# A two-layer tanh product turned inside out: weight blocks outside, 512-token blocks inside

## The chip, the cores and the metric

One Trainium2 chip, one of its eight cores. The metric is the device time of one execution in microseconds (us); lower is better. The core has a matmul engine (PE, with its weight loads shown as PEld), a vector engine (DVE), a scalar engine (ACT), a general engine (POOL) and a sync engine (SP) that issues the DMAs here. PE adds into PSUM, which has eight banks of 512 fp32 columns for each of 128 partitions; everything else lies in SBUF or in device memory.

## The reference

Attention over 4 batches, 8 heads, 576 tokens and 64 columns a head, then two MoE-like products over the 2304 tokens of all batches:

```python
x = attention(q, k, v, s)                        # 2304 x 512
gate = 1 / (1 + exp(-(x @ w_gate)))              # 512 -> 1536
y = (gate * (x @ w_val)) @ w_out                 # 1536 -> 512
h = y @ w_in                                     # 512 -> 2048   (the tanh product)
out = (h - tanh(h)) @ w_out2                     # 2048 -> 512
```

## The kernel before, in words

All is fp32. For the large products each operand is split into a high part, rounded to the matmul's type, and a low part, the rest; a product is then three matmuls: high by high, low weight by high tokens, high weight by low tokens. Weights arrive as 64-bit numbers and are converted on chip (`Conversion`: ACT scales the upper words into `tmp`, DVE joins the lower words in, lines 82 and 83, ACT writes the high part, line 124, POOL the low part, line 114; each `tick` does one step of three blocks that follow each other). Matmuls of 128 rows by 128 weight columns stream the tokens as columns; every one has a weight load of its own.

The order of work on each engine is the order in which the program writes it (`manual_schedule`); an engine runs its instructions in that order, and SP its DMAs. Waits between engines follow from the tiles that instructions write and read.

The stages, in order:

1. Attention, with the first half of the first MoE (gate and value, `gscr` in device memory) worked in between, to 536.9 us.
2. The first MoE's output product, `y`. The loop runs over six blocks of 384 tokens, inside over 12 weight blocks `won`: 72 steps of 12 matmuls. `gload` fetches a tile of gated values four steps ahead, `gsplit` splits it two steps ahead (ACT line 730, DVE line 731). Four PSUM banks collect a block and the next block uses the other four. At a block's end ACT copies them to `y`, which holds all tokens in fp32 (line 796). In this stage the 16 blocks of `w_in` are also converted, into `big`, where all of them stay.
3. The tanh product. The loop runs over eight blocks of 288 tokens, inside over 16 weight blocks: 128 steps of `hmm`, each 12 matmuls into one of the eight banks in turn, then tanh by ACT (line 829), the difference by DVE (line 830) and a store to `g2scr`. `ysplit` splits the next block of `y`, out of SBUF, half a block ahead (lines 773 and 774). `w_out2` is converted here in eight pairs (`PairConversion`, 120 steps spread over 104 steps of the loop); three pairs stay on chip in `WO`, five go to device memory through `wst` and come back as `wload`.
4. The last product, by a seven-multiplication scheme over halves: 40 steps (`dsteps`) of five token blocks by eight pairs of weight blocks. `sload` fetches the tanh product's rows back from `g2scr` (line 854), `sprep` makes seven combinations `sh` and `sl` in slots of one tile each (POOL lines 867 and 869, DVE 868, 871, 872 and 874, ACT 870 and 873), and 42 matmuls of 256 columns follow (lines 957 to 959; 21 of them in the last block). Seven banks collect; `drain` adds them up and stores. `sprep` runs two steps ahead of its use and `sload` two further.

In stage 3 the loads `wload` of pairs 3 and 4 are issued at steps 118 and 122, into the memory of `big`; pairs 5, 6 and 7 follow after the first three steps of stage 4. The buffers of stage 4 lie where `y` was (`d_open`).

Of the kernel before, what the change touches and what calls it, by code (L numbers as in the profile page):

```python
# [16 lines left out]
NT, DM = B * S, H * D  # L17
KD = DM // 128
M1, M2 = 1536 // 128, 2048 // 128
BLK = 384  # L20
NBLK = NT // BLK
Q0 = (0, 128, 256, 384, 448)
GRP = ((0, 256, (0, 1)), (256, 320, (2, 3, 4)))
MASK = -(2.0 ** 33)
# [13 lines left out]
TR2 = 16  # L38
MP = M2 // 2
ND = 3  # L40
HBLK = 288
NHB = NT // HBLK
TB = 256
DG = 2
NSB = -(-(NT // 2) // TB)
# [18 lines left out]
def attention_moe_moe2(ctx: ExitStack, tc: tile.TileContext, kqT, v, s, wg, wv, wo, win, wo2, out):  # L64
# [8 lines left out]
    def bank(i, shape):  # L73
        return psum.tile(shape, F, tag=f"bank{i}", name=f"bank{i}")
# [644 lines left out]
    def gload(i):  # L719
        if i < len(order):  # L720
            blk, m = order[i]
            G_[i] = gs.tile([128, BLK], F, tag="g", name="g", bufs=5)
            SP.dma_start(out=G_[i], in_=gscr[m][:, blk * BLK:(blk + 1) * BLK])

    def gsplit(i):
        if i < len(order):
            raw = G_[i]
            gh = gs.tile([128, BLK], R, tag="gh", name="gh")
            gl = gs.tile([128, BLK], R, tag="gl", name="gl")
# [18 lines left out]
    a_left.close()  # L748

    w2 = ctx.enter_context(tc.tile_pool(name="w2", bufs=1, side="left"))  # L750
    big = [w2.tile([128, 2, 7, 256], R, tag=f"w{q}", name=f"big{q}") for q in range(MP - ND)]

    def win_part(k):
        return big[k // 7].rearrange("p a b c -> p (a b c)")[:, (k % 7) * 512:(k % 7) * 512 + 512]

    winn = [[win_part(2 * m + p) for p in range(2)] for m in range(M2)]
    ys = ctx.enter_context(tc.tile_pool(name="ys", bufs=2, side="left"))
    y_left = ExitStack()
    yp = y_left.enter_context(tc.tile_pool(name="yp", bufs=1, side="left"))
    y = yp.tile([128, KD, NT], F, name="y")  # L760
    jobs = [(win[m].bitcast(U).rearrange("p k c -> p (k c)"), *winn[m]) for m in range(M2)]
    cv3 = b_right.enter_context(tc.tile_pool(name="cv3", bufs=2, side="right"))
    cvt = Conversion(cv3, jobs, 2, 3)
    Y_ = {}

    def ysplit(blk):
        if blk < NHB:
            Y_[blk] = []
            for d in range(KD):
                yh = ys.tile([128, HBLK], R, tag=f"yh{d}", name="yh")  # L770
                yl = ys.tile([128, HBLK], R, tag=f"yl{d}", name="yl")
                src = y[:, d, blk * HBLK:(blk + 1) * HBLK]
                ACT.activation(out=yh, in_=src, func=AF.Copy)
                DVE.tensor_tensor(out=yl, in0=src, in1=yh.bitcast(F), op=ALU.subtract)
                Y_[blk].append((yh, yl))

    for i, (blk, m) in enumerate(order):
        if m == 0:
            acc = [bank(4 * (blk % 2) + d, [128, BLK]) for d in range(KD)]
        gload(i + 4)  # L780
        gsplit(i + 2)
        gh, gl = G_.pop(i)
        for d in range(KD):
            c = slice(d * 128, d * 128 + 128)
            PE.matmul(acc[d], won[m][0][:, c], gh, start=(m == 0), stop=False)  # L785
            PE.matmul(acc[d], won[m][1][:, c], gh, start=False, stop=False)  # L786
        for d in range(KD):
            c = slice(d * 128, d * 128 + 128)
            PE.matmul(acc[d], won[m][0][:, c], gl, start=False, stop=(m == M1 - 1))  # L789
        if i % 3 == 2:  # L790
            cvt.tick()
        if i == len(order) - 3:
            ysplit(0)
        if m == M1 - 1:
            for d in range(KD):
                ACT.activation(out=y[:, d, blk * BLK:(blk + 1) * BLK], in_=acc[d], func=AF.Copy, scale=0.5)
    cvt.finish(len(cvt.jobs) - 1)
    b_right.close()


    wd = ctx.enter_context(tc.tile_pool(name="wd", bufs=1, side="right"))
    fp = ctx.enter_context(tc.tile_pool(name="fp", bufs=2, side="right"))
    c_right = ExitStack()
    cv4 = c_right.enter_context(tc.tile_pool(name="cv4", bufs=2, side="right"))
    WO = {p: wd.tile([128, 2, 7, 256], R, tag=f"w{p}", name=f"wo2{p}") for p in range(ND)}
    DP = {}
    S_ = {"i": 0}
# [4 lines left out]
        w = cv4.tile([128, 2, 7, 256], R, tag="wst", name="wst", bufs=1)  # L812
        return w[:, 0], w[:, 1], lambda: SP.dma_start(out=w2scr[p], in_=w.bitcast(F))

    order = [(blk, m) for blk in range(NHB) for m in range(M2)]

    def hmm(i):
        blk, m = order[i]
        ps = bank(i % 8, [128, HBLK])
        wh, wl = winn[m]  # L820
        for k in range(KD):
            c = slice(k * 128, k * 128 + 128)
            PE.matmul(ps, wh[:, c], Y_[blk][k][0], start=(k == 0), stop=False)  # L823
            PE.matmul(ps, wl[:, c], Y_[blk][k][0], start=False, stop=False)  # L824
        for k in range(KD):
            c = slice(k * 128, k * 128 + 128)
            PE.matmul(ps, wh[:, c], Y_[blk][k][1], start=False, stop=(k == KD - 1))  # L827
        th = fp.tile([128, HBLK], F, tag="th2", name="th2", bufs=6)
        ACT.activation(out=th, in_=ps, func=AF.Tanh)  # L829
        DVE.tensor_tensor(out=th, in0=ps, in1=th, op=ALU.subtract)  # L830
        SP.dma_start(out=g2scr[m][:, blk * HBLK:(blk + 1) * HBLK], in_=th)

    def dwidth(s):
        return min(TB, NT // 2 - s * TB)

    def d_open():
        y_left.close()
        DP["g"] = ctx.enter_context(tc.tile_pool(name="dg", bufs=2, side="left"))
        DP["s"] = ctx.enter_context(tc.tile_pool(name="ds", bufs=2, side="right"))
        for i in range(DG):  # L840
            sload(i)
# [34 lines left out]
        S_["s", i] = sh, sl  # L876

    def wload(p):
        WO[p] = w2.tile([128, 2, 7, 256], R, tag=f"w{p - ND}", name=f"wo2{p}")
        SP.dma_start(out=WO[p].bitcast(F), in_=w2scr[p])  # L880

    cvt = PairConversion(cv4, [("right", [wo2[m * 128:(m + 1) * 128].bitcast(U) for m in (p, p + MP)], p)
                               for p in range(MP)], dst, POOL)
    n0, n1 = 4, len(order) - M2 - 4
    for i, (blk, m) in enumerate(order):
        hmm(i)
        if m == M2 // 2:
            ysplit(blk + 1)
        if n0 <= i < n1:
            for _ in range((i + 1 - n0) * len(cvt.steps) // (n1 - n0) - (i - n0) * len(cvt.steps) // (n1 - n0)):  # L890
                cvt.tick()
        if i == n1:
            cvt.finish(MP - 1)
            cvt.keep()
            c_right.close()
        if i == len(order) - M2 - 2:
            d_open()
        if i == len(order) - 8 or i == len(order) - 4:
            sprep()
        if blk == NHB - 1:  # L900
            if m in (6, 10):
                wload(ND + (m == 10))


    dsteps = [(s, p) for s in range(NSB) for p in range(MP)]
# [102 lines left out]
```

## Time and profile before

| | us |
|---|---|
| median of 3 runs (lowest, highest) | 1080.03 (1079.19, 1080.19) |
| profiled execution, its time | 1079.23 |
| its span, first to last instruction | 1077.3 |
| mean granted PE clock in the profile, share of full | 0.995 |
| start of stage 2, 3, 4 (first matmul) | 536.92, 686.92, 890.45 |

The time of an execution and its span differ by 1.9 us, which lie around the instructions that the profile records. PE is busy in 97% of the span; "busy" there includes the pipelined end of each matmul, so that the durations of single matmuls overlap, and the time from one start to the next is what one costs.

### The profile page before, as it was taken

How to read it: one execution, taken by the hardware profiler on the slowest of the kernel's cores; microseconds unless marked ns; L12 is line 12 of the kernel's file. 1: busy time of each engine (PE TensorE's matmuls, PEld its weight loads, DVE VectorE, ACT ScalarE, POOL GpSimd, SP SyncE). 2: the span in 40 equal slices, each digit the busy share in tenths (PEclk: the TensorE clock that was granted, in tenths of full speed). 3: DMA queues.
4: the chain of work that ended last, by engine and by line, in shares of the span. 5: the costliest groups of instructions: out<-in, count | busy, mean ns of one | idle time of the engine just before them, and what ended most of it. 6: DMA issues, size and time to landing. Idle time of an engine off the chain costs nothing.

```text
span 1077.3 us, 22002 instructions
## 1 busy us (share of the span) xinstructions
PE 1042.4 (97%) x7612; PEld 1016.4 (94%) x7612; DVE 670.7 (62%) x1635; ACT 546.8 (51%) x1289; POOL 462.2 (43%) x606
## 2 busy tenths in 40 slices
PE   7888999999999999999999999999999999999997
PEld 5787999898999999989999999999999999999997
DVE  6786566777776777654545652254454446777875
ACT  6776466666665666643445443344444433433332
POOL 3676465666566566632402210033333314263442
PEclk9999999999999999999999999999999999999999
DMA  6774446657564656615465543245357589534433
GB/s 205 225 237 111 116 135 186 178 152 169 143 178 132 169 153 163 136 41 189 157 208 183 177 153 96 77 133 171 132 196 281 195 294 344 177 108 148 140 96 99
DMA packets 119790, 177.24 MB, mean 165 GB/s; under 512 B 16960, under 2 KB 98368, under 8 KB 118400
## 3 DMA queue, kind: packets, MB, share of 16 engines
q1 hardware_dynamic: 119680, 175.85, 53.9%
q8 instruction: 60, 0.98, 0.4%
q14 instruction: 50, 0.41, 0.1%
HBM read 128.79 MB, written 47.00 MB: 163 GB/s over the span
## 4 chain that ended last, share of the span: by engine, by line
PE 84%; DVE 5%; issue 3%; DMA 3%; ACT 3%; POOL 1%; SPq 0%; POOLq 0%; DVEq 0%; ACTq 0%
PE bank L526 8%; PE bank L527 8%; PE bank L530 8%; PE bank L824 6%; PE bank L827 6%; PE bank L823 6%; PE bank L959 5%; PE bank L958 5%; PE bank L467 5%; PE bank L957 5%; PE bank L785 5%; PE bank L789 5%; PE bank L786 5%; PE bank L428 4%; PE bank L372 2%
## 5 line engine op out<-in xcount | busy, mean ns | idle before, releaser
L959 PE MATMUL bank<-wo,sl 128*128 128x256 f32 x504 | 142.6, 283 | 0.8 <-DVE sl L872 0.8
L957 PE MATMUL bank<-wo,sh 128*128 128x256 f32 x504 | 141.9, 281 | 0.2 <-ACT sh L870 0.2
L958 PE MATMUL bank<-wo,sh 128*128 128x256 f32 x504 | 141.8, 281 | 0.0
L823 PE MATMUL bank<-yh,big 128*128 128x288 f32 x512 | 139.6, 294 | 0.0
L824 PE MATMUL bank<-yh,big 128*128 128x288 f32 x512 | 139.6, 295 | 0.0
L446 ACT ACTIVATE pth<-bank 128x512 fp32r<-128x512 f32 (+2 forms) x128 | 59.5, 465 | 145.1 <-PE bank L467 86.5
L830 DVE TENSOR_TENSOR th<-bank,th 128x288 f32<-128x288 f32 x128 | 57.6, 456 | 113.6 <-ACT th L829 112.6
L447 DVE TENSOR_TENSOR ptl<-bank,pth 128x512 fp32r<-128x512 f32 (+2 forms) x128 | 66.6, 521 | 67.6 <-PE bank L467 35.5
L829 ACT ACTIVATE th<-bank 128x288 f32<-128x288 f32 x128 | 51.9, 410 | 101.3 <-PE bank L827 97.6
L398 ACT ACTIVATE sp<-sp,nm 128x576 f32<-128x576 f32 (+2 forms) x160 | 95.6, 598 | 7.6 <-DVE nm L391 7.5
L959 PEld LDWEIGHTS bank<-wo,sl 128*128 128x128 f32 x504 | 95.3, 189 | 1.8 <-DVE sl L872 1.0
L824 PEld LDWEIGHTS bank<-yh,big 128*128 128x128 f32 x512 | 96.1, 188 | 0.0
L823 PEld LDWEIGHTS bank<-yh,big 128*128 128x128 f32 x512 | 96.0, 187 | 0.0
L957 PEld LDWEIGHTS bank<-wo,sh 128*128 128x128 f32 x504 | 95.3, 189 | 0.4 <-ACT sh L870 0.4
L958 PEld LDWEIGHTS bank<-wo,sh 128*128 128x128 f32 x504 | 95.3, 189 | 0.0
L428 PE MATMUL bank<-ident,sp 128*128 128x128 f32 (+1 forms) x480 | 74.1, 263 | 20.3 <-POOL sp L414 7.8
L867 POOL TENSOR_TENSOR s<-g 128x256 f32<-128x256 f32 (+1 forms) x40 | 37.4, 934 | 125.9 <-DMA g<-h 103.4
L827 PE MATMUL bank<-yl,big 128*128 128x288 f32 x512 | 88.6, 294 | 0.0
L731 DVE TENSOR_TENSOR gl<-g,gh 128x384 fp32r<-128x384 f32 x72 | 40.0, 557 | 75.9 <-PE bank L789 48.1
L428 PEld LDWEIGHTS bank<-ident,sp 128*128 128x128 f32 (+1 forms) x480 | 51.8, 140 | 32.7 <-POOL sp L414 14.5
L730 ACT ACTIVATE gh<-g 128x384 fp32r<-128x384 f32 x72 | 37.3, 529 | 80.6 <-PE bank L786 73.9
L414 POOL TENSOR_SCALAR sp<-sp,r 128x512 f32<-128x512 f32 (+1 forms) x90 | 57.1, 635 | 48.6 <-DVE r L407 34.6
(377 smaller groups left out, 3207.4 us busy)
## 6 DMA issues: line engine op xcount, KB each, us to landing
h<-th SPq DMA_DIRECT2D x128, 144.0 KB, 2.2
kq<-in_kq SPq DMA_DIRECT2D x32, 448.0 KB, 4.0
raw<-in_wo SPq DMA_DIRECT2D x28, 512.0 KB, 4.8
g<-g SPq DMA_DIRECT2D x72, 192.0 KB, 2.6
g<-h SPq DMA_DIRECT2D x72, 128.0 KB, 2.4
w<-wst SPq DMA_DIRECT2D x5, 1792.0 KB, 6.4
wo<-w SPq DMA_DIRECT2D x5, 1792.0 KB, 8.2
cbc<-cum SPq DMA_DIRECT2D x32, 256.0 KB, 5.5
```

The costliest lines, as they stand in the source:

```text
L398: ACT.activation(out=e["sp"], in_=e["sp"], func=AF.Exp, scale=-1.0, bias=e["m"], accum_out=e["sum"])
L428: PE.transpose(ps[:, j, :], e["sp"][p0:128, c:c + 128], ident[p0:128, p0:128])
L447: DVE.tensor_tensor(out=pl[:, js, o:o + n], in0=e["tr"], in1=ph[:, js, o:o + n].bitcast(F), op=ALU.subtract)
L526: PE.matmul(ps, wh[:, c], xh[:, k], start=(k == 0), stop=False)
L527: PE.matmul(ps, wl[:, c], xh[:, k], start=False, stop=False)
L530: PE.matmul(ps, wh[:, c], xl[:, k], start=False, stop=(k == KD - 1))
L823: PE.matmul(ps, wh[:, c], Y_[blk][k][0], start=(k == 0), stop=False)
L824: PE.matmul(ps, wl[:, c], Y_[blk][k][0], start=False, stop=False)
L827: PE.matmul(ps, wh[:, c], Y_[blk][k][1], start=False, stop=(k == KD - 1))
L957: PE.matmul(o, sh[:, g, c], w[:, 0, f], start=(p == 0 and t == 0), stop=False)
L958: PE.matmul(o, sh[:, g, c], w[:, 1, f], start=False, stop=False)
L959: PE.matmul(o, sl[:, g, c], w[:, 0, f], start=False, stop=(p == MP - 1 and t == nt - 1))
```

## The change

Stage 2 takes its tokens in blocks of 512 (four of them and one of 256), 60 steps instead of 72. Its banks are drained straight into the split form: ACT writes the high part out of PSUM with the scale 0.5, DVE the rest out of PSUM; `y` in fp32, `ysplit` and its tiles are gone, and the split `y` of all tokens stays on chip (`Y_`). Of `w_in` four blocks are converted in stage 2 (six ticks), into a ring of four.

Stage 3 has the weight blocks outside and the five token blocks inside (for the last two weight blocks the token blocks are outside and the two weights inside): 80 steps instead of 128. The 12 later ticks of the conversion stand behind the second token block of each weight block from the second on; each overwrites the ring's slot of the weight block that ended before. The weight blocks come in the order 0, 8, 1, 9, ..., so that the pairs which stage 4 needs first are done first. The 120 steps of `PairConversion` are spread over 62 steps instead of 104. `d_open` stands at step 68, `sprep` as before 8 and 4 steps from the end, and the loads of pairs 3 to 6 at steps 72, 74, 76 and 78, each into the memory of a token block of `Y_` that is read no more, pair 7 behind the last step, into the ring's memory. Tiles of stage 4's sums move to other memory. Stages 1 and 4 are otherwise as they were.

The diff, cut:

```diff
-BLK = 384
-NBLK = NT // BLK
+BLK = 512
+BLKS = [(a, min(BLK, NT - a)) for a in range(0, NT, BLK)]
+NBLK = len(BLKS)
+NW = 4
...
-    big = [w2.tile([128, 2, 7, 256], R, tag=f"w{q}", name=f"big{q}") for q in range(MP - ND)]
...
-    winn = [[win_part(2 * m + p) for p in range(2)] for m in range(M2)]
-    ys = ctx.enter_context(tc.tile_pool(name="ys", bufs=2, side="left"))
-    y_left = ExitStack()
-    yp = y_left.enter_context(tc.tile_pool(name="yp", bufs=1, side="left"))
-    y = yp.tile([128, KD, NT], F, name="y")
-    jobs = [(win[m].bitcast(U).rearrange("p k c -> p (k c)"), *winn[m]) for m in range(M2)]
-    cv3 = b_right.enter_context(tc.tile_pool(name="cv3", bufs=2, side="right"))
+    Y_ = []
+    for blk in range(NBLK - 1):
+        yt = w2.tile([128, 2, KD, BLK], R, tag=f"w{blk}", name=f"y{blk}")
+        Y_.append([[yt[:, p, d] for d in range(KD)] for p in range(2)])
+    yt = [[w2.tile([128, 2, 256], R, tag=f"o{p}{d}", name=f"y4{p}{d}") for d in range(2)] for p in range(2)]
+    Y_.append([[yt[p][d // 2][:, d % 2] for d in range(KD)] for p in range(2)])
+    ring = w2.tile([128, NW, 2, 512], R, tag="ring", name="ring")
+    MO = [m for p in range(MP) for m in (p, p + MP)]
+    cv_left = ExitStack()
+    cv3 = cv_left.enter_context(tc.tile_pool(name="cv3", bufs=2, side="left"))
+    jobs = [(win[m].bitcast(U).rearrange("p k c -> p (k c)"), ring[:, j % NW, 0], ring[:, j % NW, 1])
+            for j, m in enumerate(MO)]
     cvt = Conversion(cv3, jobs, 2, 3)
-    Y_ = {}
-
-    def ysplit(blk):
-        if blk < NHB:
-            Y_[blk] = []
-            for d in range(KD):
-                yh = ys.tile([128, HBLK], R, tag=f"yh{d}", name="yh")
-                yl = ys.tile([128, HBLK], R, tag=f"yl{d}", name="yl")
-                src = y[:, d, blk * HBLK:(blk + 1) * HBLK]
-                ACT.activation(out=yh, in_=src, func=AF.Copy)
-                DVE.tensor_tensor(out=yl, in0=src, in1=yh.bitcast(F), op=ALU.subtract)
-                Y_[blk].append((yh, yl))
...
+        w = BLKS[blk][1]
         if m == 0:
-            acc = [bank(4 * (blk % 2) + d, [128, BLK]) for d in range(KD)]
+            acc = [bank((1 + 4 * (blk % 2 == 0) + d) % 8, [128, w]) for d in range(KD)]
...
-        if i % 3 == 2:
+        if i % 8 == 5 and cvt.ticks < NW + 2:
             cvt.tick()
-        if i == len(order) - 3:
-            ysplit(0)
         if m == M1 - 1:
             for d in range(KD):
-                ACT.activation(out=y[:, d, blk * BLK:(blk + 1) * BLK], in_=acc[d], func=AF.Copy, scale=0.5)
-    cvt.finish(len(cvt.jobs) - 1)
+                yh, yl = (Y_[blk][p][d] for p in range(2))
+                ACT.activation(out=yh, in_=acc[d], func=AF.Copy, scale=0.5)
+                DVE.scalar_tensor_tensor(out=yl, in0=acc[d], scalar=0.5, in1=yh.bitcast(F),
+                                         op0=ALU.mult, op1=ALU.subtract)
...
-    order = [(blk, m) for blk in range(NHB) for m in range(M2)]
+    order = [(j, blk) for j in range(M2 - 2) for blk in range(NBLK)]
+    order += [(j, blk) for blk in range(NBLK) for j in (M2 - 2, M2 - 1)]
 
     def hmm(i):
-        blk, m = order[i]
-        ps = bank(i % 8, [128, HBLK])
-        wh, wl = winn[m]
+        j, blk = order[i]
+        a, w = BLKS[blk]
+        ps = bank((i + 1) % 8, [128, w])
+        wh, wl = (ring[:, j % NW, p] for p in range(2))
+        yh, yl = Y_[blk]
         for k in range(KD):
...
-        th = fp.tile([128, HBLK], F, tag="th2", name="th2", bufs=6)
+            PE.matmul(ps, wh[:, c], yl[k], start=False, stop=(k == KD - 1))
+        th = fp.tile([128, BLK], F, tag=f"th{i % 6}", name="th2")[:, :w]
         ACT.activation(out=th, in_=ps, func=AF.Tanh)
         DVE.tensor_tensor(out=th, in0=ps, in1=th, op=ALU.subtract)
-        SP.dma_start(out=g2scr[m][:, blk * HBLK:(blk + 1) * HBLK], in_=th)
+        SP.dma_start(out=g2scr[MO[j]][:, a:a + w], in_=th)
...
     def d_open():
-        y_left.close()
+        cv_left.close()
...
     def wload(p):
-        WO[p] = w2.tile([128, 2, 7, 256], R, tag=f"w{p - ND}", name=f"wo2{p}")
+        WO[p] = w2.tile([128, 2, 7, 256], R, tag=f"w{p - ND}" if p < MP - 1 else "ring", name=f"wo2{p}")
         SP.dma_start(out=WO[p].bitcast(F), in_=w2scr[p])
...
-    for i, (blk, m) in enumerate(order):
+    n0, n1 = 4, 66
+    n2 = len(order) - 2 * NBLK
+    for i, (j, blk) in enumerate(order):
         hmm(i)
-        if m == M2 // 2:
-            ysplit(blk + 1)
+        if i < n2 and blk == 1 and j >= 1 and wcv.ticks < M2 + 2:
+            wcv.tick()
...
-        if i == len(order) - M2 - 2:
+        if i == n1 + 2:
...
-        if blk == NHB - 1:
-            if m in (6, 10):
-                wload(ND + (m == 10))
+        if i > n2 and (i - n2) % 2 == 0:
+            wload(ND + (i - n2) // 2 - 1)
...
-            R_["c1"] = otile("yh6", w)
+            R_["c1"] = otile("o00", w)
             ACT.activation(out=R_["c1"], in_=a, func=AF.Copy)
         elif n == 2:
-            ostore(s, True, 0, dadd(("yh0", "yh1")[par], a, R_["c1"], w), w)
+            ostore(s, True, 0, dadd(("th0", "th1")[par], a, R_["c1"], w), w)
...
+    wload(MP - 1)
     for i, (s, p) in enumerate(dsteps):
...
         sprep()
-        if i + ND + 2 < MP:
-            wload(i + ND + 2)
```

## Rows read from the trace of the kernel before

**Rows 1.** The page's part 1: busy time, share of the span, instructions.

```profile
PE 1042.4 (97%) x7612; PEld 1016.4 (94%) x7612; DVE 670.7 (62%) x1635; ACT 546.8 (51%) x1289; POOL 462.2 (43%) x606
```

**Rows 2.** Windows of three stages and four saturated microseconds; columns in the first line.

```profile
core 0: us, PE busy (x) PEld busy (x) DVE busy (x) ACT busy (x) POOL busy (x), PEclk, DMA share, GB/s
560.00:685.00 125.00, 125.00 (x723) 125.00 (x722) 63.35 (x91) 54.40 (x111) 20.04 (x15) 1.00 0.46 138
711.00:887.00 176.00, 176.00 (x1330) 176.00 (x1329) 78.17 (x169) 75.67 (x167) 55.45 (x47) 1.00 0.58 203
904.00:908.00 4.00, 4.00 (x36) 4.00 (x35) 2.81 (x5) 1.80 (x2) 0.78 (x2) 1.00 1.01 393
910.00:1040.00 130.00, 130.00 (x1098) 130.00 (x1097) 102.62 (x126) 49.25 (x55) 57.22 (x53) 1.00 0.49 150
```

**Rows 3.** Waits of the matmul engine from 495 us: total, times, longest.

```profile
PE bank L959 <- DVE sl L872: 0.8, 1, 0.8
```

**Rows 4.** Timeline of PE where stages meet: start, us, engine, line, shapes.

```profile
536.92 0.33 PE L785 MATMUL bank<-gh,wo0h 128*128 128x384 f32 x1
...
537.72 0.44 PE L785 MATMUL bank<-gh,wo0h 128*128 128x384 f32 x1
...
686.92 0.30 PE L823 MATMUL bank<-yh,big 128*128 128x288 f32 x1
...
890.45 0.28 PE L957 MATMUL bank<-wo,sh 128*128 128x256 f32 x1
```

**Rows 5.** Timeline of PE in attention: a 512-wide matmul and its follower, twice.

```profile
211.15 0.39 PE L373 MATMUL bank<-kl,qs 128*128 128x512 f32 x1
211.38 0.28 PE L526 MATMUL bank<-xh,w03h 128*128 128x256 f32 x1
...
301.86 0.39 PE L373 MATMUL bank<-kl,qs 128*128 128x512 f32 x1
302.08 0.31 PE L526 MATMUL bank<-xh,w06h 128*128 128x320 f32 x1
```

**Rows 6.** Groups by form, first MoE's output product (536.9 to 686.9 us).

```profile
L731 DVE TENSOR_TENSOR gl<-g,gh 128x384 fp32r<-128x384 f32 x70 | 38.9, 557 | 72.3 <-PE bank L789 48.1 <-ACT gh L730 24.1
L730 ACT ACTIVATE gh<-g 128x384 fp32r<-128x384 f32 x69 | 35.9, 530 | 79.3 <-PE bank L786 73.9 <-DMA g<-g 4.6 <-PE bank L789 0.8
...
L114 POOL TENSOR_TENSOR big<-tmp,big 128x512 fp32r<-128x512 f32 x16 | 21.3, 1333 | 97.3 <-ACT big L124 97.3
...
L78 ACT ACTIVATE tmp<-raw 128x512 f32<-128x512 f32 x16 | 10.5, 659 | 0.6 <-DMA raw<-in_win 0.5
L124 ACT ACTIVATE big<-tmp 128x512 fp32r<-128x512 f32 x16 | 9.9, 616 | 0.0
```

**Rows 7.** Groups by form, tanh product (686.9 to 890.4 us).

```profile
L829 ACT ACTIVATE th<-bank 128x288 f32<-128x288 f32 x127 | 51.5, 410 | 100.1 <-PE bank L827 96.4 <-DMA h<-th 3.5
...
L774 DVE TENSOR_TENSOR yl<-y,yh 128x288 fp32r<-128x288 f32 x28 | 13.4, 540 | 0.0
```

**Rows 8.** Groups by form, 512 wide out of PSUM (0 to 536 us).

```profile
L447 DVE TENSOR_TENSOR ptl<-bank,pth 128x512 fp32r<-128x512 f32 x32 | 22.1, 691 | 19.7 <-ACT pth L446 19.3
...
L446 ACT ACTIVATE pth<-bank 128x512 fp32r<-128x512 f32 x32 | 19.1, 598 | 28.1 <-PE bank L428 28.1
```

**Rows 9.** Who released line 959's engine: us, times.

```profile
  DVE sl L874: 0.5, 3
```

**Rows 10.** The page's part 6: DMA issues, KB, us to landing.

```profile
wo<-w SPq DMA_DIRECT2D x5, 1792.0 KB, 8.2
...
raw<-in_win SPq DMA_DIRECT2D x16, 512.0 KB, 3.5
```

**Rows 11.** Timeline of SP, POOL and DVE early in the last stage.

```profile
897.50 1.38 SPq L854 DMA_DIRECT2D g<-h  x3
...
901.97 1.10 POOL L867 TENSOR_TENSOR s<-g 128x256 f32<-128x256 f32 x1 [2.26 <-DMA g<-h]
...
907.51 1.23 DVE L874 TENSOR_TENSOR sl<-s,sh 128x1024 fp32r<-128x1024 f32 x1
```

More of the change, by code (lines that the diff above doesn't have):

```diff
@@ L40 @@
 ND = 3
-HBLK = 288
-NHB = NT // HBLK
 TB = 256
@@ L721, in gload @@
             blk, m = order[i]
-            G_[i] = gs.tile([128, BLK], F, tag="g", name="g", bufs=5)
-            SP.dma_start(out=G_[i], in_=gscr[m][:, blk * BLK:(blk + 1) * BLK])
+            a, w = BLKS[blk]
+            G_[i] = gs.tile([128, BLK], F, tag="g", name="g", bufs=5)[:, :w]
+            SP.dma_start(out=G_[i], in_=gscr[m][:, a:a + w])
     def gsplit(i):
@@ L727, in gsplit @@
             raw = G_[i]
-            gh = gs.tile([128, BLK], R, tag="gh", name="gh")
-            gl = gs.tile([128, BLK], R, tag="gl", name="gl")
+            w = BLKS[order[i][0]][1]
+            gh = gs.tile([128, BLK], R, tag="gh", name="gh")[:, :w]
+            gl = gs.tile([128, BLK], R, tag="gl", name="gl")[:, :w]
             ACT.activation(out=gh, in_=raw, func=AF.Copy)
@@ L750, in attention_moe_moe2 @@
     w2 = ctx.enter_context(tc.tile_pool(name="w2", bufs=1, side="left"))
-    big = [w2.tile([128, 2, 7, 256], R, tag=f"w{q}", name=f"big{q}") for q in range(MP - ND)]
-    def win_part(k):
-        return big[k // 7].rearrange("p a b c -> p (a b c)")[:, (k % 7) * 512:(k % 7) * 512 + 512]
-    winn = [[win_part(2 * m + p) for p in range(2)] for m in range(M2)]
-    ys = ctx.enter_context(tc.tile_pool(name="ys", bufs=2, side="left"))
-    y_left = ExitStack()
-    yp = y_left.enter_context(tc.tile_pool(name="yp", bufs=1, side="left"))
-    y = yp.tile([128, KD, NT], F, name="y")
-    jobs = [(win[m].bitcast(U).rearrange("p k c -> p (k c)"), *winn[m]) for m in range(M2)]
-    cv3 = b_right.enter_context(tc.tile_pool(name="cv3", bufs=2, side="right"))
-    cvt = Conversion(cv3, jobs, 2, 3)
-    Y_ = {}
-    def ysplit(blk):
-        if blk < NHB:
-            Y_[blk] = []
-            for d in range(KD):
-                yh = ys.tile([128, HBLK], R, tag=f"yh{d}", name="yh")
-                yl = ys.tile([128, HBLK], R, tag=f"yl{d}", name="yl")
-                src = y[:, d, blk * HBLK:(blk + 1) * HBLK]
-                ACT.activation(out=yh, in_=src, func=AF.Copy)
-                DVE.tensor_tensor(out=yl, in0=src, in1=yh.bitcast(F), op=ALU.subtract)
-                Y_[blk].append((yh, yl))
+    Y_ = []
[10 more added lines that the diff above has]
+            for j, m in enumerate(MO)]
+    cvt = Conversion(cv3, jobs, 2, 3)
     for i, (blk, m) in enumerate(order):
+        w = BLKS[blk][1]
         if m == 0:
-            acc = [bank(4 * (blk % 2) + d, [128, BLK]) for d in range(KD)]
+            acc = [bank((1 + 4 * (blk % 2 == 0) + d) % 8, [128, w]) for d in range(KD)]
         gload(i + 4)
@@ L789, in attention_moe_moe2 @@
             PE.matmul(acc[d], won[m][0][:, c], gl, start=False, stop=(m == M1 - 1))
-        if i % 3 == 2:
+        if i % 8 == 5 and cvt.ticks < NW + 2:
             cvt.tick()
-        if i == len(order) - 3:
-            ysplit(0)
         if m == M1 - 1:
             for d in range(KD):
-                ACT.activation(out=y[:, d, blk * BLK:(blk + 1) * BLK], in_=acc[d], func=AF.Copy, scale=0.5)
-    cvt.finish(len(cvt.jobs) - 1)
+                yh, yl = (Y_[blk][p][d] for p in range(2))
+                ACT.activation(out=yh, in_=acc[d], func=AF.Copy, scale=0.5)
+                DVE.scalar_tensor_tensor(out=yl, in0=acc[d], scalar=0.5, in1=yh.bitcast(F),
+                                         op0=ALU.mult, op1=ALU.subtract)
     b_right.close()
     wd = ctx.enter_context(tc.tile_pool(name="wd", bufs=1, side="right"))
-    fp = ctx.enter_context(tc.tile_pool(name="fp", bufs=2, side="right"))
+    fp = ctx.enter_context(tc.tile_pool(name="fp", bufs=1, side="right"))
     c_right = ExitStack()
     cv4 = c_right.enter_context(tc.tile_pool(name="cv4", bufs=2, side="right"))
+    wcv = cvt
     WO = {p: wd.tile([128, 2, 7, 256], R, tag=f"w{p}", name=f"wo2{p}") for p in range(ND)}
@@ L813, in dst @@
         return w[:, 0], w[:, 1], lambda: SP.dma_start(out=w2scr[p], in_=w.bitcast(F))
-    order = [(blk, m) for blk in range(NHB) for m in range(M2)]
+    order = [(j, blk) for j in range(M2 - 2) for blk in range(NBLK)]
+    order += [(j, blk) for blk in range(NBLK) for j in (M2 - 2, M2 - 1)]
     def hmm(i):
-        blk, m = order[i]
-        ps = bank(i % 8, [128, HBLK])
-        wh, wl = winn[m]
+        j, blk = order[i]
+        a, w = BLKS[blk]
+        ps = bank((i + 1) % 8, [128, w])
+        wh, wl = (ring[:, j % NW, p] for p in range(2))
+        yh, yl = Y_[blk]
         for k in range(KD):
             c = slice(k * 128, k * 128 + 128)
-            PE.matmul(ps, wh[:, c], Y_[blk][k][0], start=(k == 0), stop=False)
-            PE.matmul(ps, wl[:, c], Y_[blk][k][0], start=False, stop=False)
+            PE.matmul(ps, wh[:, c], yh[k], start=(k == 0), stop=False)
+            PE.matmul(ps, wl[:, c], yh[k], start=False, stop=False)
         for k in range(KD):
             c = slice(k * 128, k * 128 + 128)
-            PE.matmul(ps, wh[:, c], Y_[blk][k][1], start=False, stop=(k == KD - 1))
-        th = fp.tile([128, HBLK], F, tag="th2", name="th2", bufs=6)
+            PE.matmul(ps, wh[:, c], yl[k], start=False, stop=(k == KD - 1))
+        th = fp.tile([128, BLK], F, tag=f"th{i % 6}", name="th2")[:, :w]
         ACT.activation(out=th, in_=ps, func=AF.Tanh)
         DVE.tensor_tensor(out=th, in0=ps, in1=th, op=ALU.subtract)
-        SP.dma_start(out=g2scr[m][:, blk * HBLK:(blk + 1) * HBLK], in_=th)
+        SP.dma_start(out=g2scr[MO[j]][:, a:a + w], in_=th)
     def dwidth(s):
@@ L883, in attention_moe_moe2 @@
                                for p in range(MP)], dst, POOL)
-    n0, n1 = 4, len(order) - M2 - 4
-    for i, (blk, m) in enumerate(order):
+    n0, n1 = 4, 66
+    n2 = len(order) - 2 * NBLK
+    for i, (j, blk) in enumerate(order):
         hmm(i)
-        if m == M2 // 2:
-            ysplit(blk + 1)
+        if i < n2 and blk == 1 and j >= 1 and wcv.ticks < M2 + 2:
+            wcv.tick()
         if n0 <= i < n1:
@@ L909, in otile @@
     def otile(k, w):
-        return op.tile([128, 512], F, tag=k, name="o")[:, 0:w]
+        pool = w2 if k[1:].isdigit() else fp if k[0] == "t" else op
+        return pool.tile([128, 512], F, tag=k, name="o")[:, 0:w]
     def dadd(k, x, y, w, op=ALU.add):
@@ L927, in drain @@
         if n == 1:
-            R_["c1"] = otile("yh6", w)
+            R_["c1"] = otile("o00", w)
             ACT.activation(out=R_["c1"], in_=a, func=AF.Copy)
         elif n == 2:
-            ostore(s, True, 0, dadd(("yh0", "yh1")[par], a, R_["c1"], w), w)
+            ostore(s, True, 0, dadd(("th0", "th1")[par], a, R_["c1"], w), w)
         elif n == 6:
-            R_["u2"] = dadd("yl4", a, R_["c1"], w)
+            R_["u2"] = dadd("o01", a, R_["c1"], w)
         elif n == 7:
-            R_["u3"] = dadd("yl5", a, R_["u2"], w)
+            R_["u3"] = dadd("o10", a, R_["u2"], w)
         elif n == 5:
-            ostore(s, False, 1, dadd(("yh2", "yh3")[par], a, R_["u3"], w), w)
-            R_["v"] = dadd("yl6", a, R_["u2"], w)
+            ostore(s, False, 1, dadd(("th2", "th3")[par], a, R_["u3"], w), w)
+            R_["v"] = dadd("o11", a, R_["u2"], w)
         elif n == 4:
-            ostore(s, False, 0, dadd(("yh4", "yh5")[par], a, R_["u3"], w), w)
+            ostore(s, False, 0, dadd(("th4", "th5")[par], a, R_["u3"], w), w)
         else:
-            ostore(s, True, 1, dadd(("yl0", "yl1")[par], a, R_["v"], w), w)
+            ostore(s, True, 1, dadd(("ox0", "ox1")[par], a, R_["v"], w), w)
+    wload(MP - 1)
     for i, (s, p) in enumerate(dsteps):
```

## The prediction

> **What bounds the kernel now.** I read the page's first part, then windows inside the stages that the diff touches, then the waits of PE, then PE's timeline where stages meet. The first says that PE is busy in 97% of the span and no other engine in more than 62% [rows 1]. Busy PE could still be slow PE, so the windows count: in stage 2 PE is busy in all of 125.00 us and starts 723 matmuls, 172.9 ns each; in stage 3, 1330 in 176.00 us, 132.3 ns; in stage 4, 1098 in 130.00 us, 118.4 ns, all at a granted clock of 1.00, the 2.4 GHz level [rows 2]. At one column per cycle of 2.4 GHz the 384, 288 and 256 columns take 160.0, 120.0 and 106.7 ns. What is left over is 12.9, 12.3 and 11.7 ns: each matmul pays about 12 ns that hardly depend on its width. The waits after 495 us say that PE waited almost for nothing in these stages (0.8 us the longest [rows 3]), and the timeline that one stage follows the other without a gap: stage 2 from 536.92 to 686.92, 150.0 us, stage 3 from there to 890.45, 203.5 us [rows 4]. So stages 2 and 3 are worth what their matmuls cost, and a change there must change the number of matmuls, their price, or make PE wait.
>
> **Matmuls, the term that decides.** Columns stay: 864 x 384 in stage 2 are 576 x 512 and 144 x 256; 1536 x 288 in stage 3 are 768 x 512 and 192 x 256. The matmuls fall by 144 and by 576, 720 together. At 12.5 ns each (between the three above) this is 9.0 us. The price of a 512-wide one in a row of its like is not in stages 2 to 4. Three ways to it: the three stages' 12.5 ns on top of 213.3 give 225.8; the line through 256 and 384 columns (0.426 ns a column) goes on to 227.4; and attention has single ones, whose followers start 0.23 and 0.22 us later [rows 5]. I take 226.5, and 118.4 for 256 columns.
>
> Stage 2: 576 x 0.2265 + 144 x 0.1184 = 130.5 + 17.0 = 147.5 us against 150.0: 2.5 us less. About 0.2 of these are a hitch in the first step, where whose fifth start comes 0.80 us after its first instead of 0.69, and the sixth as late again [rows 4]: its banks are those out of which the last gate products are still drained, and the new first block begins in banks 5, 6 and 7. Stage 3: 768 x 0.2265 + 192 x 0.1184 = 173.9 + 22.7 = 196.7 against 203.5: 6.8 less. Sum: 9.3 us. Over the 1344 wide matmuls each ns of their price is 1.34 us; with 0.22 us the gain would be 18 us, with 0.23 it would be 4.6. Since both followers are single starts shown to 10 ns, the line and the fixed part (227.4 and 225.8, gains of 8.1 and 10.2) are the nearer bounds.
>
> The Trainium skill (TensorE: Matmul & The Clock Gate, section "Back-to-back issue gap") gives a warm isolated gap of N/2.4 + 2.5 ns, which is 215.8 ns at 512 columns. By it the gain would be 24 us. The trace does not follow it at 384 columns, where it would give 162.5 and [rows 2] give 172.9.
>
> **Drains and splits.** `ysplit` goes (32 ACT and 32 DVE instructions; the DVE ones took 540 ns in the mean [rows 7]). Each block's four drains become one ACT and one DVE instruction out of PSUM; the nearest rows are 598 and 691 ns at 512 wide [rows 8]. ACT ends a block's four 2.4 us after it starts, and it starts three matmuls before PE ends the block, since the banks close one by one: some 2 us after. Behind them on ACT stands the split for the step after next; at 384 wide it takes 530 and 557 ns [rows 6], at 512 some 0.7 each on two engines. In 512-wide blocks PE asks for it 5.4 us (two steps) after the block, in the 256-wide last block after 2.9. There gh comes at about 2.4 and gl, which is read a microsecond later, at about 3.3: free, by half a microsecond. If it is not, it costs that once.
>
> **The ring.** Twelve conversions move from stage 2 into stage 3: ACT 659 + 616 ns, POOL 1333 ns each [rows 6], DVE two instructions. Stage 3 leaves each engine room: in 176 us DVE was busy 78, ACT 76, POOL 55 [rows 2]. The denser pair conversion (62 steps of 2.46 us, 152 us, where it had 104 of 1.59, 165 us) changes little. But a tick in stage 3 loads its raw block and scales it at once, so ACT waits for the landing, 3.5 us in the median [rows 10], and the next tanhs queue behind. The load goes out after the store of the same step, say 1.5 us after PE ended it; the tanh behind is then some 3 us late. PE feels it only when a bank is not free, eight steps on, 19 us. A slot is written three weight blocks (37 us) before it is read. Cost nothing; without the eight banks it would be 12 x 3 = 36 us.
>
> **Between the stages.** The first raw loads wait for the last gate product's weights, whose memory they take; the load for step 4 stands behind them on SP. It should land 5 us into stage 2 and is split by 7; PE needs it at 10.9. Nothing. The first product of stage 3 finds four weight blocks converted since step 45 and Y_ of blocks 0 to 3 drained; the fifth is read 10.9 us on.
>
> **The reload.** Here I see the one thin place. Loads of 1792 KB for pairs 3 to 7 were spread over steps of stage 4; now 5, 6 and 7 go out within some 2.5 us around its start T. Saturated, the queue moves 393 GB/s [rows 2], so each takes 4.7 us, and the three are in at about T + 13.4. The load for the fifth step of stage 4 goes out at T + 7.05 as before (897.50 less 890.45 [rows 11]) and lands behind them, at about T + 15.5, where before POOL could begin with it at 901.97, T + 11.5. Two POOL instructions, one of DVE, one of ACT and one of DVE follow each other; the first took 1.10 and the last 1.23 us [rows 11], so I estimate 5.7 for the five, which brings the last slot to about T + 21.2. PE enters that step at T + 20 and reaches the first of these slots after 14 more matmuls, at T + 21.7. So nothing, with 0.5 us in hand; every microsecond beyond costs one, once, and 5 us if a transfer is slow (this load landed in 7.3 to 10.4 us before, 8.2 in the median [rows 10]).
>
> So 1079.23 - 9.3 = 1069.9 against the profiled execution. The median of the runs is 0.8 above that execution; by it 1070.7. I put the time between, 1070.3.
>
> **Rivals.**
> The reload makes PE wait: 1 to 5 us, 1072 to 1075. For it: the saturated queue. Against it: one step only, and it has half a microsecond in hand by the mean rate. 0.16.
>
> The ring is ordered as one tile, and slower than before: were writes of one slot held against reads of another, PE could not start the product behind a tick before tanh (0.6), copy (0.62) and POOL's low part (1.33) were done, 2.6 us and a handover, 12 times: 33 us, 1103 us. It decides from 0.8 us a tick on. Against it: slots of the tile `sl` release PE singly, by line 872 [rows 3] and by line 874 [rows 9]. 0.05.
>
> A wide matmul costs two narrow ones: 2 x 118.4 = 236.8, 1344 x 10.3 ns = 13.8 us back, 1083.7; with 233.4 ns the change does nothing. Against it: [rows 5]. 0.03.
>
> The fixed part vanishes at full width: were the 12 ns a weight load that a longer matmul hides, 512 columns would cost 213.3 ns and the time be 1069.9 - 1344 x 0.0132 = 1052. Against it: the part does not shrink from 256 to 384 columns [rows 2]. 0.04. The Trainium skill's gap named above would lead near there, to 1055.5.
>
> **Numbers.** My forecast has 0.72, with a range of its own from 1067.5 to 1072.5 (the two bounds of the wide price and the 0.8 us between execution and median). With the reload's share the range goes from 1066 to 1075.5 and leaves out some 0.14. What a measurement can tell here from no change is about 0.2%, 2.2 us; faster by more than that is forecast, reload and vanishing part, 0.92; slower the ring and most of the double price, 0.07; the rest, 0.01, is same.
>
> **What would show it.** Starts of 512-wide matmuls 226 ns apart in both stages; stage 2 in 147.5 us, stage 3 in 196.7; no PE wait in stage 3 behind a tick; step five of stage 4 on time, its load landed by T + 16. A price under 222 or over 230 ns, or a wait of PE over 3 us anywhere between 537 us and the end of stage 4's first block, makes the prediction wrong.

## The result and the profile after

The changed kernel takes 1091.95 us in the median of 4 runs (1091.01 to 1092.56) against 1079.61 us of the kernel before on the same chip (4 runs): a ratio of 1.0113, 95% interval 1.0096 to 1.0131. It is slower by 12.3 us, where 9.3 us less were forecast. The profiled execution took 1092.56 us with a span of 1090.8.

The page's busy times and granted clock in 40 slices:

```profile
PE 1040.5 (95%) x6892; PEld 960.9 (88%) x6892; DVE 660.7 (61%) x1563; ACT 520.8 (48%) x1193; POOL 470.6 (43%) x606
...
PEclk9999999999999999999999999999998998999999
```

PE works 2 us less than before [rows 1] in a span that is 13.5 us longer, and its clock is no longer full in every slice. So the matmuls may well be cheaper; time is lost between them. The chain that ended last shows the price (start, us, engine, line), in rows that stand one step of 12 matmuls apart, first in stage 2, then in stage 3:

```profile
540.84 0.91 PE bank L780 x4
543.56 0.91 PE bank L780 x4
...
688.71 0.91 PE bank L822 x4
691.43 0.91 PE bank L822 x4
```

2.72 us over 12 are 226.7 ns in both stages. The borders of the stages on PE's timeline, which answer to [rows 4]:

```profile
538.82 0.39 PE L776 MATMUL bank<-gh,wo0h 128*128 128x512 f32 x1
...
686.69 0.39 PE L818 MATMUL bank<-y,ring 128*128 128x512 f32 x1
...
890.78 0.28 PE L954 MATMUL bank<-wo,sh 128*128 128x256 f32 x1
```

| us | stage 1 to | stage 2 | stage 3 | stage 4 to the span's end |
|---|---|---|---|---|
| before | 536.92 | 150.00 | 203.53 | 186.85 |
| after | 538.82 | 147.87 | 204.09 | 200.0 |
| forecast | no change | 147.5 | 196.7 | 186.9 |

Stage 2 came as forecast. Stage 3 kept nothing of its gain, stage 4 lost 13.1 us, and stage 1, whose program is the same, ended 1.9 us later. PE's waits after 537 us (total, times, longest), where the largest before was 0.8 us [rows 3]:

```profile
PE bank L954 <- ACT sh L865: 8.6, 1, 8.6
PE bank L818 <- DVE th L825: 4.2, 1, 4.2
PE bank L956 <- DVE sl L867: 3.1, 2, 2.3
PE bank L954 <- DVE th L825: 0.3, 1, 0.3
```

The reader is to see three places: the product of stage 3 that waits for line 825, DVE's difference that frees a bank; line 954, the first matmul of a step of stage 4; and line 956 in the same step. Windows around both places (the columns are those of [rows 2]):

```profile
core 0: us, PE busy (x) PEld busy (x) DVE busy (x) ACT busy (x) POOL busy (x), PEclk, DMA share, GB/s
...
822.00:826.00 4.00, 0.61 (x6) 0.40 (x4) 0.00 (x0) 1.11 (x3) 0.00 (x0) 0.83 0.97 355
826.00:830.00 4.00, 3.19 (x8) 2.54 (x9) 2.72 (x5) 3.96 (x8) 3.16 (x2) 0.50 0.65 243
830.00:834.00 4.00, 4.00 (x16) 3.27 (x15) 2.96 (x3) 0.00 (x0) 2.45 (x2) 0.81 0.81 261
910.00:914.00 4.00, 1.83 (x16) 1.63 (x14) 0.00 (x0) 0.00 (x0) 0.00 (x0) 1.00 1.03 428
914.00:918.00 4.00, 0.00 (x0) 0.00 (x0) 0.00 (x0) 0.00 (x0) 0.00 (x0) 0.85 0.98 380
918.00:922.00 4.00, 0.80 (x2) 0.50 (x2) 1.30 (x3) 0.84 (x1) 2.29 (x4) 0.50 0.31 101
922.00:926.00 4.00, 2.50 (x11) 2.50 (x12) 4.00 (x6) 2.50 (x3) 0.64 (x1) 0.50 0.30 74
```

PE stands still from 822 and again from 911 us. In both places the granted clock falls while PE is idle (0.83 and 0.85 in the windows of the idle time), reads 0.50, the 1.2 GHz level, in the window after, and is full again only some microseconds after the work resumes. The DMA engines are at 0.97 or more in the windows from 822 and from 910 to 918 us, in which PE does least.

What stage 3 waits for shows in ACT's timeline (in brackets the idle time before and what ended it):

```profile
705.21 0.62 ACT L124 ACTIVATE ring<-tmp 128x512 fp32r<-128x512 f32 x1
710.00 0.67 ACT L78 ACTIVATE tmp<-raw 128x512 f32<-128x512 f32 x1 [4.17 <-DMA raw<-in_win]
...
800.52 0.63 ACT L124 ACTIVATE ring<-tmp 128x512 fp32r<-128x512 f32 x1
806.33 0.66 ACT L78 ACTIVATE tmp<-raw 128x512 f32<-128x512 f32 x1 [5.17 <-DMA raw<-in_win]
...
812.81 0.63 ACT L124 ACTIVATE ring<-tmp 128x512 fp32r<-128x512 f32 x1
824.89 0.66 ACT L78 ACTIVATE tmp<-raw 128x512 f32<-128x512 f32 x1 [11.45 <-DMA raw<-in_win]
```

Line 124 is ACT's first instruction of a tick. The n-th tick of stage 3 stands behind the second product of weight block n, which PE ends at 686.69 + n x 12.34 + 5.44 us (12.34 us is what the four wide products and the narrow one of a weight block take). For n = 1 this is 704.5, and ACT reaches the tick 0.7 us later; for n = 8 it is 790.9 and ACT 9.7 us late; for n = 9 it is 803.2 and ACT 9.6 late. There it then waits 11.45 us for the raw block. That makes 21 us, more than the eight banks cover. The lag did not grow evenly: by the same sum ACT came to ticks 1 to 9 by 0.7, 0.7, 0.7, 3.6, 0.7, 3.7, 6.5, 9.7 and 9.6 us late. So it caught up within a round at first, and from the sixth tick on it did not. SP's timeline says why the raw block of the ninth tick is late:

```profile
809.17 6.71 SPq L826 DMA_DIRECT2D h<-th  x4
815.98 0.38 SPq L805 DMA_DIRECT2D w<-wst  x1
...
816.91 1.09 SPq L105 DMA_DIRECT2D raw<-in_win  x1
...
896.21 5.14 SPq L826 DMA_DIRECT2D h<-th  x2
901.69 0.32 SPq L875 DMA_DIRECT2D wo<-w  x1
902.34 0.32 SPq L826 DMA_DIRECT2D h<-th  x1
902.75 0.38 SPq L875 DMA_DIRECT2D wo<-w  x1
903.24 21.65 SPq L849 DMA_DIRECT2D g<-h  x9
```

SP issues in order. The stores before the load wait for DVE's differences of tanhs that stand behind the previous ticks on the late ACT, so the load goes out late too, and behind a store of 1792 KB issued 0.9 us ahead. It lands after 8.0 us; the median of the ten loads is 4.2. In the lower rows the same queue holds the last tanh stores, the reloads of pairs 6 and 7, and only then, at 903.24, the loads of the tanh rows for the fifth step of stage 4. ACT's two largest waits for DMA in stage 3:

```profile
ACT tmp L78 <- DMA raw<-in_win: 61.0, 10, 11.5
ACT wst L196 <- DMA w<-wst: 22.3, 3, 9.7
```

### The profile page after: what moved, and what is told of

It reads as the page before. It is cut to its first block, busy times and chain, and to the rows that moved or that the text cites. A ratio compares the mean times of both kernels' runs of the same rounds, so it can differ in the third digit from the quotient of the medians.

```text
span 1090.8 us, 20116 instructions
## 1 busy us (share of the span) xinstructions
PE 1040.5 (95%) x6892; PEld 960.9 (88%) x6892; DVE 660.7 (61%) x1563; ACT 520.8 (48%) x1193; POOL 470.6 (43%) x606
## 4 chain that ended last, share of the span: by engine, by line
PE 72%; DMA 9%; DVE 7%; issue 5%; ACT 3%; POOL 2%; SPq 1%; DVEq 0%; ACTq 0%; POOLq 0%
PE bank L526 8%; PE bank L527 8%; PE bank L530 8%; PE bank L467 5%; PE bank L776 5%; PE bank L780 5%; PE bank L777 5%; PE bank L956 4%; PE bank L955 4%; PE bank L954 4%; PE bank L428 4%; PE bank L819 3%; PE bank L818 3%; PE bank L822 3%; PE bank L372 2%
## 5 line engine op out<-in xcount | busy, mean ns | idle before, releaser
L818 PE MATMUL bank<-y,ring 128*128 128x512 f32 (+1 forms) x320 | 116.8, 372 | 4.2 <-DVE th L825 4.2
L819 PE MATMUL bank<-y,ring 128*128 128x512 f32 (+1 forms) x320 | 116.8, 372 | 0.0
L825 DVE TENSOR_TENSOR th<-bank,th 128x512 f32<-128x512 f32 (+1 forms) x80 | 48.5, 632 | 98.0 <-ACT th L824 94.8
L114 POOL TENSOR_TENSOR ring<-tmp,ring 128x512 fp32r<-128x512 f32 x16 | 23.0, 1438 | 193.2 <-ACT ring L124 169.9
L733 DVE TENSOR_TENSOR gl<-g,gh 128x512 fp32r<-128x512 f32 (+1 forms) x60 | 37.7, 636 | 84.6 <-PE bank L780 62.3
L865 ACT ACTIVATE sh<-g 128x768 fp32r<-128x768 f32 (+1 forms) x40 | 31.2, 781 | 103.1 <-PE bank L955 53.6
L822 PE MATMUL bank<-y,ring 128*128 128x512 f32 (+1 forms) x320 | 79.2, 370 | 0.0
L78 ACT ACTIVATE tmp<-raw 128x512 f32<-128x512 f32 x59 | 38.6, 664 | 83.1 <-DMA raw<-in_win 61.0
L732 ACT ACTIVATE gh<-g 128x512 fp32r<-128x512 f32 (+1 forms) x60 | 35.0, 591 | 90.3 <-PE bank L777 82.5
```

The costliest lines, as they stand in the source:

```text
L818: PE.matmul(ps, wh[:, c], yh[k], start=(k == 0), stop=False)
L819: PE.matmul(ps, wl[:, c], yh[k], start=False, stop=False)
L822: PE.matmul(ps, wh[:, c], yl[k], start=False, stop=(k == KD - 1))
```

## The experiments

Seven kernels ran, in two groups, each beside the kernel before on the same chip (1080.79 us in the median for the first four, 1080.04 for the last three). The first three undo the suspected waits singly and together.

**e1: Raw loads a tick ahead.**

```diff
-    cvt = Conversion(cv3, jobs, 2, 3)
+    cvt = Conversion(cv3, jobs, 3, 3)
```

> The changed kernel with one more buffer for the raw blocks of the ring's conversion, so that each load goes out one tick (a weight block, 12.3 us) before ACT scales it. Theory A: ACT waits 61 us in stage 3 for loads issued in the same tick, and the tanhs behind them come so late that PE stalls 4.2 us and its clock falls; then ACT's wait for these loads is under 10 us, PE has no stall in stage 3, the stage takes 197 us instead of 204.1, and the last tanhs are on time. The reload's stall in stage 4 stays, perhaps smaller: 1075 to 1085 us. Rival B: the denser pair conversion, whose staging tile waits for its store (22.3 us of ACT's waits), makes the lag; then stage 3 stays at 202 us or more and the kernel at 1088 to 1092.

1079.84 us, ratio 0.9990 (0.9976 to 1.0004). ACT has no wait for these loads any more, PE none in stage 3, and the stage takes 197.43 us. Theory A holds and B falls: ACT still waits 18.2 us for the staging tile's store. Stage 4 takes 192.5 us. There the fifth step's rows go out at 891.16, 7.4 us after the stage began at 883.73, as early as before, and yet POOL can begin with them only at 905.20. SP's timeline, POOL's, and three windows:

```profile
882.74 0.61 SPq L875 DMA_DIRECT2D wo<-w  x1
...
886.63 0.32 SPq L875 DMA_DIRECT2D wo<-w  x1
...
887.69 1.42 SPq L875 DMA_DIRECT2D wo<-w  x1
891.16 37.55 SPq L849 DMA_DIRECT2D g<-h  x21
```

```profile
905.20 0.72 POOL L862 TENSOR_TENSOR s<-g 128x256 f32<-128x256 f32 x1 [14.91 <-DMA g<-h]
```

```profile
880.00:884.00 4.00, 4.00 (x32) 3.84 (x31) 3.36 (x5) 2.00 (x4) 0.00 (x0) 1.00 1.07 450
...
900.00:904.00 4.00, 3.95 (x34) 3.74 (x32) 0.00 (x0) 0.00 (x0) 0.00 (x0) 1.00 0.99 370
...
908.00:912.00 4.00, 2.85 (x13) 2.85 (x14) 3.77 (x5) 2.58 (x3) 0.28 (x1) 0.63 0.30 80
```

The queue is saturated all the time from the stage's start to 904 us (a DMA share of 0.96 or more in every window), at up to 450 GB/s, and PE, which waits 4.7 us in the fifth step, sees a clock of 0.63 afterwards. Against the version with both edits below, the reloads cost 7 us here with every tanh on time.

**e2: Reloads spread.** Pairs 3 and 4 as in the change, pairs 5 to 7 behind the first three steps of stage 4.

```diff
-        if i > n2 and (i - n2) % 2 == 0:
+        if i in (n2 + 2, n2 + 4):
             wload(ND + (i - n2) // 2 - 1)
...
-    wload(MP - 1)
...
         sprep()
+        if i + ND + 2 < MP:
+            wload(i + ND + 2)
```

> The changed kernel with the reloads of pairs 5, 6 and 7 behind the first, second and third step of stage 4, after that step's load of tanh rows, as in the kernel before. Theory C: the stall of 8.6 and 2.3 us in the fifth step of stage 4 comes from those three reloads standing ahead of that step's rows in the DMA queue; then the stall is gone and stage 4 takes 187 to 188 us instead of 200.0, 1079 to 1081 us in all. Rival D: the rows come late because the last tanh stores hold SP up; then stage 4 keeps 5 us or more of stall and the kernel takes 1085 us or more.

1080.85 us, ratio 0.9994 (0.9981 to 1.0007). PE's waits:

```profile
PE bank L818 <- DVE th L825: 4.0, 1, 4.0
PE bank L955 <- DVE sl L867: 2.1, 3, 0.8
```

The stall in the fifth step is gone; 2.3 us in small pieces remain, and stage 4 takes 189.8 us. D as stated (5 us or more of stall) falls; C holds for the stall, but stage 4 stays some 2 us above its forecast. The tanhs are still late here (stage 3 takes 204.3 us and its stall of 4.0 us stays; the last tanh starts 4.9 us after the first matmul of stage 4, where it starts 0.2 us after it with the raw loads ahead), and the rest of the loss goes with them, as the next run shows.

**e3: Both.**

> Both edits in the changed kernel. Theories A and C together: stage 2 147.9, stage 3 197, stage 4 187 us, so 8.5 to 9.5 us under the kernel before, 1070 to 1072. Rivals B or D: 1076 or more.

1071.14 us, ratio 0.9905 (0.9887 to 0.9923): stage 2 in 147.86, stage 3 in 197.44, stage 4 in 185.6 us. PE's only wait after 537 us is

```profile
PE bank L955 <- DVE sl L867: 0.8, 1, 0.8
```

This is the change without its two stalls, 9.6 us under the kernel before, and the fastest version that ran.

**e4: Stage 2 alone.** The kernel before with `BLK = 512` in stage 2, the drains still into `y`, `bank((i + 1) % 8)` in stage 3 and four buffers for the gated tiles.

> The kernel before with stage 2 alone in blocks of 512 tokens (y still in fp32, all of w_in converted there, stage 3 as before, the banks turned by one; one buffer fewer for the gated tiles, for space). The price of a matmul as predicted: stage 2 takes 147.7 us instead of 150.0, and the kernel 1077.3, 2.3 us (0.2%) less. If a stage keeps what it gains only where stage 3's splits are not in the way: 1079 to 1080.

1078.49 us, ratio 0.9974 (0.9962 to 0.9985): 2.3 us less in the medians. Stage 2 takes 147.87 us, stage 3 203.52 as before. The price of a wide matmul is worth what was worked out, where nothing else is moved.

The last three ask how the stalls come about.

**e5: The load one step before its tick**, in the same two buffers, with the reloads spread.

```diff
+        if i < n2 and blk == 0 and j >= 1:
+            wcv.load()
         if i < n2 and blk == 1 and j >= 1 and wcv.ticks < M2 + 2:
             wcv.tick()
```

> The changed kernel with the reloads spread (as in e2) and the ring's raw load issued one step of the loop before the tick that scales it, in the same two buffers. Theory A (the late loads make ACT fall behind until a bank is missing): a head start of one step, 2.7 us, on each of ten waits cuts ACT's 60 us to some 30, ACT stays within eight banks of PE, PE has no wait in stage 3, the stage takes 197.4 to 198 us and the kernel 1071 to 1073. Rival E (one long wait of 11 us, behind a store of 1792 KB, makes the stall, whatever the others are): the long wait stays near 9 us, PE still waits 2 us or more, stage 3 takes 200 us or more, the kernel 1075 or more.

1073.75 us, ratio 0.9933 (0.9909 to 0.9957). ACT's waits in stage 3, then the longest of them on its timeline:

```profile
ACT tmp L78 <- DMA raw<-in_win: 34.8, 10, 7.5
ACT wst L196 <- DMA w<-wst: 25.7, 4, 11.1
```

```profile
841.55 0.85 ACT L196 ACTIVATE wst<-tmp 128x768 fp32r<-128x768 f32 x1 [11.06 <-DMA w<-wst]
...
842.77 0.62 ACT L124 ACTIVATE ring<-tmp 128x512 fp32r<-128x512 f32 x1
```

ACT still has a wait of 11.06 us, as long as the one that stopped PE in the changed kernel, and PE has none: stage 3 takes 197.43 us. The tick that stands behind this wait starts at 842.77, 13.2 us after PE ended its product (688.39 + 11 x 12.34 + 5.44 = 829.6), and 13.2 is inside the eight banks. So one long wait is not enough, and the lag that earlier ticks leave decides. Rival E's forecast falls too, though less sharply: the wait that it named, for the raw load, became 7.5 us and not the 9 that it supposed. The kernel's median is 2.6 us above that of both edits (in another group of runs); in the profile stage 4 took 188.6 us, with waits of 2.1 us. The last tanh starts 3.2 us after the first matmul of stage 4 here, 4.9 with the reloads spread alone and 0.2 with both edits, and stage 4 is longer in the same order: 188.6, 189.8 and 185.6 us. How the late tanhs lead to these small waits was not followed up.

**e6: Two staging tiles** (`bufs=2` for `wst`), reloads spread, raw loads as in the change.

> The changed kernel with the reloads spread (as in e2) and two staging tiles instead of one for the converted pairs; the raw loads go out late as in the changed kernel. Theory A: ACT's 22 us of waiting for the staging tile's store fall below 5, its 60 us for the raw loads stay at 50 to 60, and PE keeps a stall of 2 to 4 us in stage 3 (202 us or more; kernel 1077 to 1081). Rival B (the staging tile is the cause): no stall, 197 to 198 us, kernel 1071 to 1073.

1076.30 us, ratio 0.9965 (0.9954 to 0.9976). ACT no longer waits for the store, but for the raw loads as long as ever, and the stall is there (ACT's wait, then PE's):

```profile
ACT tmp L78 <- DMA raw<-in_win: 66.5, 10, 11.5
```

```profile
PE bank L818 <- DVE th L825: 3.9, 1, 3.9
```

Stage 3 takes 203.93 us. Rival B falls for stage 3. The kernel is still 4.5 us faster than with one tile (medians 1080.85 and 1076.30, in two groups), and in the profiles this lies in stage 4: 185.4 us against 189.8. Here the last tanh starts 0.2 us after the first matmul of stage 4, as with both edits. So the staging tile's wait, which does not make the stall of stage 3, is part of what makes the last tanhs late.

**e7: One reload later.** Raw loads a tick ahead, pair 7 behind the second step of stage 4, pairs 5 and 6 as in the change.

```diff
-    wload(MP - 1)
...
         sprep()
+        if i == 1:
+            wload(MP - 1)
```

> The changed kernel with the raw loads a tick ahead (as in e1) and one of the three late reloads, pair 7's, behind the second step of stage 4 instead of ahead of the first. Theory C by queue length: one reload of 1792 KB less ahead of the fifth step's rows is some 4.5 us; PE's 4.7 us of waits there fall to 0 to 1, stage 4 takes 185.5 to 187 us instead of 192.5, the kernel 1071 to 1073. If the order of the rows behind pairs 5 and 6 alone is too late: stage 4 at 189 us or more, 1075 or more.

1073.50 us, ratio 0.9945 (0.9924 to 0.9966). Stage 4 takes 186.9 us instead of 192.5, and the larger of PE's two waits is

```profile
PE bank L955 <- DVE sl L867: 1.5, 2, 0.8
```

One transfer of 1792 KB moved out from ahead of the rows is worth 5.6 us of the stage: the rows land by 17.0 us after its start instead of 21.3.

| us | stage 2 | stage 3 | stage 4 | median |
|---|---|---|---|---|
| changed kernel | 147.87 | 204.09 | 200.0 | 1091.95 |
| raw loads ahead | 147.87 | 197.43 | 192.5 | 1079.84 |
| reloads spread | 147.87 | 204.30 | 189.8 | 1080.85 |
| both | 147.86 | 197.44 | 185.6 | 1071.14 |
| load a step before, reloads spread | 147.84 | 197.43 | 188.6 | 1073.75 |
| two staging tiles, reloads spread | 147.87 | 203.93 | 185.4 | 1076.30 |
| raw ahead, one reload later | 147.83 | 197.44 | 186.9 | 1073.50 |

## Why the prediction was wrong

**Right: the matmuls.** 226.7 ns at 512 columns, where 226.5 was taken; 147.87 and 197.4 us for stages 2 and 3, where 147.5 and 196.7 were worked out. The run with both edits, 1071.14 us, lies 0.8 us above the forecast, and stage 2 alone brought its 2.3 us. That it lies so near is in part luck: stages 2 and 3 are together 1.1 us over what was worked out, and stage 4 is 1.2 us under the kernel before for a reason that was not forecast. Neither a double price nor a vanishing part showed. Drains, splits and the border of stages 2 and 3 cost nothing, as forecast: no PE wait stands there.

**Wrong: the ring, put at "Cost nothing".** The mechanism was in the prediction: ACT waits for a raw block in the tick that loads it, tanhs queue behind, PE feels it eight steps on, at 19 us. The step that failed is the lag: I let each tick make the next tanh 3 us late and took it as made good before the next tick. ACT, however, lost 61 us to these waits, 22 to the staging tile's store and 10 to POOL in a stage of 204. At ticks 2, 3 and 5 the lag had been made good as supposed; from the sixth on it had not, and it grew from 0.7 to 9.7 us before the longest wait took it past 19. Being late gave ACT no head start on the load, because the load goes out on SP behind stores that wait for ACT's own tanhs: each of the ten loads was issued 0.6 us or more after ACT stood ready for it, in two ticks 3.0 and 3.5 us, 12 of the 61 us together. The other 49 us are the landings, 3.5 us in the median of stage 2 [rows 10] and 4.2 here; three took 6.0 to 8.0 us, the longest of them the one behind the store of 1792 KB. With the loads a round ahead the staging tile's waits remained and PE had no stall, and with two staging tiles the stall stayed; so it is the raw loads that the step had wrong. Cost: 204.1 - 197.4 = 6.7 us, of which 4.2 are PE's wait; the rest lies where the clock is at its lower level (0.50 in the window from 826 us).

**Wrong by size: "The reload."** The place was right, the fifth step of stage 4, and so was the order of the transfers. Two terms were mis-sized. The queue: I counted three reloads and took it as empty before them. With the tanhs on time POOL could begin with the rows 21.5 us after the stage began, not 15.5: pair 4 and the tanh rows and stores behind it held the queue for the stage's first 4.9 us, and pairs 5, 6 and 7 landed at 9.7, 14.9 and 19.6 us, not by 13.4. The price of one reload was right: each landed 4 to 5 us behind what was ahead of it. The fuller queue alone takes 192.5 - 185.6 = 6.9 us with its clock, where "5 us if a transfer is slow" was the bound. And the start: in the changed kernel the rows went out 12.5 us into the stage (903.24 - 890.78), not 7.05. SP's own waits from 886 to 904 us say what held it:

```profile
SPq L826 <- DMA wo<-w: 4.4, 1, 4.4
SPq L849 <- DMA wo<-w: 3.6, 1, 3.6
...
SPq L826 <- DVE th L825: 0.7, 3, 0.3
```

It waited 8.0 us for the landing of reloads and 0.7 us for differences of tanhs. A store whose difference DVE had ended at 892.9 us went out at 901.02, just after pair 4's reload had landed at 900.96; eight transfers were out until then. The late tanhs come in one step earlier: the reloads of pairs 3 and 4 stand among the last tanh stores on SP, so they went out 4.4 and 2.8 us ahead of the stage's start, where with the tanhs on time it was 11.9 and 9.1.

Ticks and reloads together took 200.0 - 185.6 = 14.4 us; the late tanhs alone 189.8 - 185.6 = 4.2, so 3.3 us come only where both meet (each from one profile).

**The rivals.** The reload rival named the right place and priced it too low: 1 to 5 us, where the reloads take 6.9 with the tanhs on time and the two together 14.4. The ring rival that ends on the slower side had the wrong mechanism: nothing in any run speaks for slots that are ordered as one tile, since the lag comes from the loads and goes with them. What was missing was a rival in which ACT's lag adds up over the ticks.

**Stage 1** ended between 536.42 and 540.55 us in the nine profiles with an unchanged program, so its 1.9 us are not the change's; in the profile after, the first products of attention already come 2.3 us later than before. What makes the start vary stays open. So does the 1.2 us by which stage 4 of the version with both edits is shorter than before; half of it lies behind the last matmul (3.8 us to the span's end, 4.4 before).

## What to carry to other kernels

An engine that runs in order and waits inside a loop is not covered because each single wait is shorter than the buffers behind it: add up its waits over a period and ask whether it has caught up before the next one, above all where its own lateness delays the transfer it waits for. Issue a load at least one round ahead of the instruction that reads it, and count everything that is in a saturated queue, not only what the change adds, before a transfer is put behind it.

## What the runs showed of the hardware

A stall of PE costs more than its own length: after 4.2 us idle the granted clock read 0.50 in the next window and 0.81 in the one after, and after 8.6 us 0.50 over two windows of 4 us. In the changed kernel the idle time of PE adds up to 16.2 us, while against the version with both edits stages 3 and 4 are 21.1 us longer.

SP never has more than eight transfers out. In each of the nine traces, which hold 728 to 788 of its DMAs, every issue comes after the landing of the eighth issue before it. So a long transfer holds back not only what lands behind it, but also SP itself, and with it every store and load that comes later in SP's order (4.4 and 3.6 us in the changed kernel). What sets the eight, the chip or the way the program is built, no run shows.
